# Three of the 48 output-weight rows of a partition are loaded on their own by small DMAs, and the score sums are taken two chunks at a time

## The chip, the cores and the metric

One NeuronCore of a Trainium2 chip runs the kernel; the metric is device time of one execution in microseconds (us). The engines are PE (TensorE), DVE (VectorE), ACT (ScalarE), POOL (GpSimd) and SP (SyncE, which here only issues DMAs); sixteen DMA engines move the data. POOL and ACT can issue DMAs too.

## What is computed

One decoding step of a transformer block for 4 sequences: sliding-window attention over a cache, plus a gated feed-forward part, plus the input.

```python
x = A_x                                   # [4, 1, 640]
xn = _layernorm(x)
q = (xn @ wq)                             # 32 heads of 192
k, v = the last W = 2048 of 8192 cached positions, [4, 32, 2048, 192] each
p = softmax(q k^T * 192 ** -0.5)
attn = (p v, heads side by side) @ wo     # wo is [6144, 640]
ffn = (silu(xn @ w1) * (xn @ w3)) @ w2    # F = 1536
return x + attn + ffn
```

All inputs are bf16. The keys and values that are read are 201 MB of the 223 MB that the kernel reads.

## The kernel before

**Layout.** Partition p = 4 * head + r holds a quarter r of the window of one head. The window is cut into NU = 4 units of 512 positions, so a unit of keys or of values is one tile of 128 partitions x 128 positions x 192 numbers, 6 MB, 49,152 contiguous bytes a partition. `load` (L104 to L111) fetches such a tile by one DMA from SP into the pool `kv` of three buffers; the two last halves of values are fetched apart.

**Keys.** `keys` (L231) treats a unit in four chunks of 32 positions. DVE multiplies a chunk with the query (`mult`, L212, into one of two buffers `pr`), PE adds the 192 products down to 16 by twelve matmuls with the identity (`adder`, L219, into PSUM tile `ps`), and DVE sums the last 16 (`reduces`, L229). A list, `pend`, holds chunks whose last sum is still to be issued; `reduces` is called after the next chunk's product. After four units `chain` makes the softmax numbers.

**Values.** `values` (L264) spreads the weights into a tile `z` (DVE, L268) and multiplies it with the value tile on PE (L280). `evict` and `sort` (L288 to L298) bring a sequence's result into `oT`, [128 partitions, NI = 48, 32], the left operand of the output projection: partition p holds 48 of the 6144 rows of the attention result, and the same 48 rows of wo belong to it.

**Output weights.** Row i of partition p of wo is 640 numbers, 1,280 bytes. `wo_load` (L302) loads rows 38 to 47 into a `pr` buffer, and rows 0 to 25 and 26 to 37 (cuts 0, WM = 26, NI - WI = 38) into a `kv` buffer. `proj` (L312 to L316) adds two matmuls a row into the PSUM tile `acc`: rows 38 to 47 first, then 0 to 37.

**Feed-forward.** w1 and w3 are loaded and multiplied before the last values; w2 comes as the last three loads (8 rows, 3 rows, 1 row; L326), and its 24 matmuls (L423) are the last of PE. DVE adds the parts (L415, L416, L426), and two DMAs store the result.

**What sets the order.** PE and DVE each issue in the order of the program text (`ordered` adds the dependence). SP issues its DMAs in program order and waits in front of one until its buffer is free. `feed` issues one entry of the list `stream` for each unit that the main loop works off: cache units, then w1 and w3, the last values with wo rows 38 to 47, then the rest of wo and w2. So each of the sixteen DMA engines has a queue of SP's transfers and works through it in that order; a cache load gives each engine eight rows of 49,152 bytes.

**Start.** POOL makes the two identities and clears `oT` and others (L121 to L160), then loads x into `x_st` by two small DMAs (L125). DVE and ACT do the layer norm, and PE makes the queries as soon as wq has landed (L196, L205); ACT puts them into `qb` (L206).

The code of the functions concerned, with the profile's line numbers:

Of the kernel before, what the change touches and what calls it, by code (L numbers as in the profile page):

```python
# [10 lines left out]
FP32 = mybir.dt.float32  # L11
BF16 = mybir.dt.bfloat16
ALU = mybir.AluOpType
ACTF = mybir.ActivationFunctionType
AX = mybir.AxisListType
# [3 lines left out]
def kernel(  # L19
# [13 lines left out]
    CH: int = 32,  # L33
    R: int = 4,
    WI: int = 10,
    WM: int = 26,
    ALIGN: int = 64,
):


# [5 lines left out]
    nc = tc.nc  # L46
    P = 128
    B, Sq, D = A_x.shape
    _, H, Sk, Dh = A_k_cache.shape
# [3 lines left out]
    NJ = P  # L53
    NU = W // (NJ * R)
    NC = NJ // CH
    NK = Dh // DD
    SCALE = float(Dh) ** -0.5
    EPS = 1e-5
    NI = Dh // R
    NG = P // 32  # L60
    NH = H // NG
    QW = 2 * Dh
    NCH = 512
    DH = D // 2
# [11 lines left out]
    const = ctx.enter_context(tc.tile_pool(name="const", bufs=1))  # L76
    kvpool = ctx.enter_context(tc.tile_pool(name="kv", bufs=3))
    ppool = ctx.enter_context(tc.tile_pool(name="pr", bufs=2))
# [1 line left out]
    opool = ctx.enter_context(tc.tile_pool(name="o", bufs=1))  # L80
    small = ctx.enter_context(tc.tile_pool(name="small", bufs=2))
    ps_add = ctx.enter_context(tc.tile_pool(name="ps_add", bufs=2, space=MemoryType.PSUM))
    ps_o = ctx.enter_context(tc.tile_pool(name="ps_o", bufs=2, space=MemoryType.PSUM))
    ps_t = ctx.enter_context(tc.tile_pool(name="ps_t", bufs=3, space=MemoryType.PSUM))
    ps_acc = ctx.enter_context(tc.tile_pool(name="ps_acc", bufs=1, space=MemoryType.PSUM))

    ORDER_DEP = mybir.DependencyInfo(mybir.DependencyClass.NoSync, mybir.DependencyReason.SCHED_ONLY)
# [2 lines left out]
    def ordered(engine, inst):  # L90
        if engine in last:
            tc.add_manual_dep(inst.ins, last[engine].ins.name, ORDER_DEP, reason="issue order")
        last[engine] = inst
        return inst

    def dve(inst):
        return ordered("dve", inst)

    def pe(inst):
        return ordered("pe", inst)  # L100
# [3 lines left out]
    def load(which, b, s, n0=0, n1=NJ):  # L104
        if n0 == 0:
            kv = kvpool.tile([P, NJ, Dh], BF16, tag="kv")
            kvs[which, b, s] = kv
        p0 = Sk - W + s * NJ * R
        rows = {"k": A_k_cache, "v": A_v_cache}[which][b, :, p0:p0 + NJ * R, :].rearrange("h (r n) d -> h r n d", r=R)
        nc.sync.dma_start(out=kvs[which, b, s][:, n0:n1, :].rearrange("p n d -> p (n d)"),  # L110
                          in_=rows[:, :, n0:n1, :].rearrange("h r n d -> h r (n d)"))  # L111
# [8 lines left out]
    x_st = const.tile([64, DH], BF16, name="x_st")  # L120
    nc.gpsimd.memset(x_st[:], 0.0)  # L121

    def x_load():
        for t in range(2):
            nc.gpsimd.dma_start(out=x_st[32 * t:32 * t + B, :], in_=x_rows[:, t * DH:(t + 1) * DH])  # L125
# [7 lines left out]
    nc.sync.dma_start(out=wq1[:], in_=wq_rows[:, RV:KC, :])  # L133
    for s in range(2):
        load("k", 0, s)

    idb = const.tile([P, P], BF16, name="idb")
    make_identity(nc, idb[:])
    idf = const.tile([P, P], FP32, name="idf")
# [15 lines left out]
    at = (NH - 1) * NG * R  # L155
    for b in range(B):
        nc.vector.tensor_copy(out=qwin[:, b, at:at + NG * R].rearrange("p (g r) -> p g r", r=R),
                              in_=idf[:, b:P:32].unsqueeze(2).to_broadcast([P, NG, R]))
    oT = const.tile([P, NI, 32], BF16, name="oT")
    nc.gpsimd.memset(oT[:], 0.0)  # L160

# [23 lines left out]
    acc = ps_acc.tile([64, DH], FP32, name="acc")  # L185

    q_pss = []
    for k in range(NH // 2):
        pool, tag = (ps_add, "ps") if k < 2 else (ps_o, "o_ps")
        qp = pool.tile([P, 512], FP32, tag=tag)  # L190
        q_pss.append(qp)
    for kc in range(KC):
        wq = (wq0[:, kc, :] if kc < RV else wq1[:, 0, :]).rearrange("p (k g d) -> p k g d", g=NG, d=Dh)
        for k in range(NH // 2):
            for g in range(NG):
                pe(nc.tensor.matmul(q_pss[k][32 * g:32 * g + 32, 0:QW], lhsT=xnT[:, kc, :], rhs=wq[:, 2 * k:2 * k + 2, g, :],  # L196
                                    start=(kc == 0), stop=(kc == KC - 1)))
    for k in range(NH // 2):
        nc.scalar.copy(out=q_sb[:, 2 * k:2 * k + 2, :], in_=q_pss[k][:, 0:QW].rearrange("p (x d) -> p x d", x=2))
    qb = const.tile([P, B, Dh], BF16, name="qb")  # L200
    for b in range(B):
        bp = ps_t.tile([P, Dh], FP32, tag="t")
        for k in range(NH):
            w0 = (NH - 1 - k) * NG * R
            pe(nc.tensor.matmul(bp[:], lhsT=qwin[:, b, w0:w0 + P], rhs=q_sb[:, k, :], start=(k == 0), stop=(k == NH - 1)))  # L205
        nc.scalar.copy(out=qb[:, b, :], in_=bp[:])  # L206

    scs, es, rss, rcps, pend = {}, {}, {}, {}, []

    def mult(b, s, c):  # L210
# [2 lines left out]
                                    in1=qb[:, b, :].unsqueeze(1).to_broadcast([P, CH, Dh]), op=ALU.mult))  # L213
        return pr

    def adder(b, s, c, pr):
        ps = ps_add.tile([P, CH, DD], FP32, tag="ps")
        for kk in range(NK):
            pe(nc.tensor.matmul(ps[:], lhsT=idb[:], rhs=pr[:, :, kk * DD:(kk + 1) * DD], start=(kk == 0), stop=(kk == NK - 1)))  # L219
        pend.append((b, s, c, ps))  # L220

    def reduces():
        while pend:
            b, s, c, ps = pend.pop(0)
            if b not in scs:
                sc = small.tile([P, NU * NJ], FP32, tag="sc", bufs=1)
                scs[b] = sc
            at = s * NJ + c * CH
            dve(nc.vector.tensor_reduce(out=scs[b][:, at:at + CH], in_=ps[:], axis=AX.X, op=ALU.add))  # L229

    def keys(b, s):  # L231
        for c in range(NC):
            pr = mult(b, s, c)
            reduces()
            adder(b, s, c, pr)
# [55 lines left out]
    def sort(b):  # L291
        fp = ps_t.tile([P, NI], FP32, tag="t")
        o_ev = o_evs.pop(b)
        for c in range(R):
            for t in range(2):
                pe(nc.tensor.matmul(fp[:], lhsT=esel[:, t, R - 1 - c:R - 1 - c + P], rhs=o_ev[:, t, c * NI:(c + 1) * NI],  # L296
                                    start=(c == 0 and t == 0), stop=(c == R - 1 and t == 1)))
        nc.scalar.mul(out=oT[:, :, b:b + 1].rearrange("p i o -> p (i o)"), in_=fp[:], mul=rcps.pop(b)[:, 0:1])  # L298
# [3 lines left out]
    def wo_load(cuts, pool, tag, shape):  # L302
        wt = pool.tile(shape, BF16, tag=tag)
        flat = wt[:].rearrange("p a n -> p (a n)")
        for i0, i1 in zip(cuts, cuts[1:]):
            at = (i0 - cuts[0]) * D
            nc.sync.dma_start(out=flat[:, at:at + (i1 - i0) * D],
                              in_=A_wo.rearrange("(p i) n -> p i n", i=NI)[:, i0:i1, :].rearrange("p i n -> p (i n)"))
            for i in range(i0, i1):
                wos[i] = flat[:, at + (i - i0) * D:at + (i - i0 + 1) * D]  # L310

    def proj(i0, i1):  # L312
        for i in range(i0, i1):
            for t in range(2):
                pe(nc.tensor.matmul(acc[32 * t:32 * t + 32, :], lhsT=oT[:, i, :], rhs=wos[i][:, t * DH:(t + 1) * DH],  # L315
                                    start=(i == i0 and i0 == proj0), stop=(i == proj1)))  # L316
# [9 lines left out]
    def w2_load(i0, i1):  # L326
        if i0 == 0:
            ffn[2] = ffn["tile"][:, 2 * KC * F:2 * KC * F + NF * CF * D].rearrange("p (i n) -> p i n", n=D)
        nc.sync.dma_start(out=ffn[2][:, i0:i1, :], in_=B_w2.rearrange("(p i) n -> p i n", p=P)[:, i0:i1, :])
# [22 lines left out]
            pe(nc.tensor.transpose(out=hT_ps[:, c, :], in_=ffn["h"][0:32 * NF, c:NCH:CF], identity=idb[0:32 * NF, 0:32 * NF]))  # L352
        dve(nc.vector.tensor_copy(out=hT[:], in_=hT_ps[:]))

    proj0, proj1 = NI - WI, NI - WI - 1

    def last_values():
        for g in range(VS):
            load("v", B - 1, NU - 1, g * NJ // VS, (g + 1) * NJ // VS)
        wo_load((NI - WI, NI), ppool, "pr", [P, WI, D])  # L360

    def gates():
        ffn_load(1)
        ffn_load(3)

    def last_weights():
        wo_load((0, WM, NI - WI), kvpool, "kv", [P, NJ, Dh])
        for i0, i1 in ((0, (NF - 1) * CF), ((NF - 1) * CF, NF * CF - 1), (NF * CF - 1, NF * CF)):
            w2_load(i0, i1)

    units = [("k", 0, s) for s in range(NU)]
    for b in range(B):
        for s in range(NU):
            units += [("v", b, s)] + ([("k", b + 1, s)] if b < B - 1 else [])
    stream = [(load, u) for u in units[2:-1]] + [(gates, ()), (last_values, ()), (last_weights, ())]

    def feed():
        fn, args = stream.pop(0)
        fn(*args)

    feed()
    for which, b, s in units[:-1]:
        if which == "k":
            keys(b, s)
        else:
            if s == 0:
                reduces()
                chain(b)
            values(b, s)
        if stream:  # L390
            feed()
        if which == "k" and b > 0:
            reduces()
            if s == 0:
                rowsum(b - 1)
                if b == B // 2:
                    x_load()
            elif s == NU - 1:
                sort(b - 1)
        if which == "v" and s == NU - 1 and b < B - 1:  # L400
            evict(b)
        if which == "v" and s == 0 and b == B - 1:
            rowsum(b)
# [4 lines left out]
        values(B - 1, NU - 1, g * NJ // VS, (g + 1) * NJ // VS)  # L408
    evict(B - 1)
    sort(B - 1)  # L410
    proj(NI - WI, NI)
    proj(0, NI - WI)

    t1 = opool.tile([64, DH], BF16, tag="t1")
    dve(nc.vector.tensor_copy(out=t1[:], in_=acc[:]))  # L415
# [4 lines left out]
    for i in range(NF * CF):  # L420
        n, c = i // CF, i % CF
        for t in range(2):
            pe(nc.tensor.matmul(ff[32 * t:32 * t + 32, :], lhsT=hT[:, c, 32 * n:32 * n + 32], rhs=ffn[2][:, i, t * DH:(t + 1) * DH],  # L423
               start=(i == 0), stop=(i == NF * CF - 1)))
# [34 lines left out]
```

## Time and profile before

| what | us |
|---|---|
| median of 3 runs | 526.11 (526.09, 526.11, 526.54) |
| the profiled execution, its own time | 526.01 |
| its span, first to last instruction | 524.1 |
| PE busy | 341.9 (65%) |
| DVE busy | 300.5 (57%) |
| ACT busy | 17.8 (3%) |
| POOL busy | 4.7 (1%) |
| HBM read | 222.96 MB, 425 GB/s over the span |

The time outside the span is 526.01 - 524.1 = 1.9 us. In the page's second part the span is cut into 40 slices, with the busy share of an engine in tenths; the row DMA there is the mean share of the sixteen DMA engines. Its third part lists queues: q1 is what SP issues, q0 what POOL issues, q8 and q14 are instructions on their way to the engines. The chain of waits follows the end back to its causes. The trace also has every DMA packet: start, duration, queue and bytes, though not the number of the DMA engine that moved it; and for each DMA the sixteen times at which its completion semaphore was raised.

### The profile page before, as it was taken

To read this page: it belongs to the slowest core of one execution; us is meant where nothing else is said; L and a number is where in the kernel's file an instruction comes from. 1 tells how busy PE (TensorE), PEld (TensorE's weight loads), DVE (VectorE), ACT (ScalarE), POOL (GpSimd) and SP (SyncE) were. 2 spreads that over 40 slices of the span, in tenths; PEclk is the share of its full clock that TensorE was granted. 3 is DMA by queue.
4 is the path that set the end of the run, shared out by engine and by line. 5 is a ranking of instruction groups with operands and counts; after the bars stand their busy time and mean duration, and the time that the engine had idled before them with its cause. 6 is when DMAs were issued, how large, how long until landed. Compare 5 with 4: busy or idle time off the path is not lost.

```text
span 524.1 us, 4690 instructions
## 1 busy us (share of the span) xinstructions
PE 341.9 (65%) x2147; PEld 199.4 (38%) x2147; DVE 300.5 (57%) x189; ACT 17.8 (3%) x34; POOL 4.7 (1%) x13
## 2 busy tenths in 40 slices
PE   0507677667676776596675866686565867688447
PEld 0302233253524352363434342353324353475445
DVE  4018999876583937676564828675574839411200
ACT  2110000000000000000000000000000000001100
POOL 3000000000000000000000000000000000000000
PEclk9977999979897887889798887998797888888797
DMA  9999999999999999999999999999999999999995
GB/s 361 431 448 439 420 425 447 439 421 424 436 450 425 420 435 451 431 418 439 443 433 424 424 455 431 425 420 450 436 431 421 435 448 428 428 420 427 432 425 240
DMA packets 6299, 223.26 MB, mean 426 GB/s; under 512 B 756, under 2 KB 904, under 8 KB 1032
## 3 DMA queue, kind: packets, MB, share of 16 engines
q1 hardware_dynamic: 6200, 222.96, 98.6%
q8 instruction: 16, 0.26, 0.2%
q14 instruction: 3, 0.02, 0.0%
q0 software_dynamic: 64, 0.01, 0.0%
q10 hardware_dynamic: 16, 0.01, 0.0%
HBM read 222.96 MB, written 0.01 MB: 425 GB/s over the span
## 4 chain that ended last, share of the span: by engine, by line
DMA 43%; DVE 29%; PE 25%; issue 1%; ACT 1%; SPq 0%; DVEq 0%; ACTq 0%
DMA kv<-in_A_k_cache_dram 38%; DVE pr L212 21%; PE o_ps L280 12%; PE ps L219 9%; DMA wt<-in_A_wo_dram 6%; DVE z L268 4%; DVE sc L229 4%; PE acc L315 2%; PE fp L296 1%; ACT e L252 1%; PE ft L423 0%; PE mt L247 0%; DVE gmax L244 0%; DVE gmq L246 0%; PE mt L242 0%
## 5 line engine op out<-in xcount | busy, mean ns | idle before, releaser
L212 DVE TENSOR_TENSOR pr<-kv,qb 128x6144 bf16<-128x6144 bf16 x64 | 213.4, 3351 | 104.7 <-DMA kv<-in_A_k_cache_dram 104.7
L219 PE MATMUL ps<-pr,idb 128*128 128x512 bf16 x768 | 194.1, 409 | 96.8 <-DVE pr L212 96.8
L219 PEld LDWEIGHTS <-idb 128*128 128x128 bf16 x768 | 79.5, 104 | 208.6 <-issue 122.6
L280 PE MATMUL o_ps<-kv,z 128*64 128x384 bf16 x1024 | 115.1, 396 | 50.6 <-DVE z L268 45.4
L280 PEld LDWEIGHTS <-z 128*64 128x64 bf16 x1024 | 94.5, 197 | 70.6 <-DVE z L268 53.0
L229 DVE TENSOR_REDUCE sc<-ps 128x32 f32<-128x512 f32 x64 | 43.9, 687 | 47.3 <-PE ps L219 47.2
L268 DVE TENSOR_TENSOR z<-e,selz 128x4096 bf16<-128x4096 bf16 (+1 forms) x17 | 36.7, 2158 | 18.2 <-PE o_ps L280 14.5
L315 PE MATMUL acc<-wt,oT 128*32 128x320 bf16 x96 | 9.5, 371 | 6.7 <-DMA wt<-in_A_wo_dram 6.1
L415 DVE CAST t<-acc 64x320 bf16<-64x320 f32 x1 | 0.5, 483 | 22.3 <-PE acc L315 22.3
L288 ACT COPY o_ev<-o_ps 128x384 f32<-128x384 f32 x4 | 1.9, 479 | 289.5 <-PE o_ps L280 289.5
L196 PE MATMUL qp<-wq,xnT 128*32 128x384 bf16 x80 | 5.2, 440 | 7.9 <-DMA wq<-in_A_wq_dram 7.9
L315 PEld LDWEIGHTS <-oT 128*32 128x32 bf16 x96 | 6.5, 118 | 9.5 <-issue 7.0
L296 PEld LDWEIGHTS fp<-o_ev,esel 128*128 128x128 f32 x64 | 7.7, 192 | 1.3 <-ACT o_ev L288 0.9
L296 PE MATMUL fp<-o_ev,esel 128*128 128x48 f32 x64 | 7.6, 272 | 0.6 <-ACT o_ev L288 0.6
L344 DVE TENSOR_TENSOR t_bf<-sg,t_bf 96x512 bf16<-96x512 bf16 x1 | 0.4, 420 | 11.5 <-ACT t_bf L338 11.5
L180 PE MATMUL xnT_ps<-idb,scratch 4*128 4x4 bf16 x5 | 0.4, 178 | 9.9 <-DVE scratch L176 9.9
L196 PEld LDWEIGHTS <-xnT 128*32 128x32 bf16 x80 | 3.1, 128 | 9.8 <-issue 7.5
L252 ACT ACTIVATE e<-sc,negm 128x512 bf16<-128x512 f32 x4 | 2.9, 721 | 80.5 <-DVE negm L249 80.5
L259 DVE RECIPROCAL rcp<-tb 128x1 f32<-128x1 f32 x4 | 0.6, 160 | 7.4 <-PE tb L257 7.4
L298 ACT ACTIVATE oT<-fp,rcp 128x48 bf16<-128x48 f32 x4 | 1.9, 468 | 64.9 <-PE fp L296 64.9
L180 PEld LDWEIGHTS <-scratch 4*128 4x128 bf16 x5 | 0.3, 125 | 9.9 <-DVE scratch L176 9.9
L205 PE MATMUL bp<-scratch 128*128 128x192 bf16 x32 | 3.3, 245 | 0.3
(60 smaller groups left out, 48.1 us busy)
## 6 DMA issues: line engine op xcount, KB each, us to landing
kv<-in_A_k_cache_dram SPq DMA_DIRECT2D x16, 6144.0 KB, 28.2
kv<-in_A_v_cache_dram SPq DMA_DIRECT2D x15, 6144.0 KB, 27.3
wq<-in_A_wq_dram SPq DMA_DIRECT2D x1, 6144.0 KB, 17.4
kv<-in_A_v_cache_dram SPq DMA_DIRECT2D x2, 3072.0 KB
wt<-in_A_wo_dram SPq DMA_DIRECT2D x1, 4160.0 KB, 29.4
ft<-in_B_w_dram SPq DMA_DIRECT2D x2, 1920.0 KB, 18.2
wt<-in_A_wo_dram SPq DMA_DIRECT2D x1, 1920.0 KB
wt<-in_A_wo_dram SPq DMA_DIRECT2D x1, 1600.0 KB, 27.8
```

Source lines behind the costliest of these rows:

```text
L196: pe(nc.tensor.matmul(q_pss[k][32 * g:32 * g + 32, 0:QW], lhsT=xnT[:, kc, :], rhs=wq[:, 2 * k:2 * k + 2, g, :], start=(kc == 0), stop=(kc ...
L205: pe(nc.tensor.matmul(bp[:], lhsT=qwin[:, b, w0:w0 + P], rhs=q_sb[:, k, :], start=(k == 0), stop=(k == NH - 1)))
L212: dve(nc.vector.tensor_tensor(out=pr[:], in0=kvs["k", b, s][:, c * CH:(c + 1) * CH, :], in1=qb[:, b, :].unsqueeze(1).to_broadcast([P, CH, ...
L219: pe(nc.tensor.matmul(ps[:], lhsT=idb[:], rhs=pr[:, :, kk * DD:(kk + 1) * DD], start=(kk == 0), stop=(kk == NK - 1)))
L229: dve(nc.vector.tensor_reduce(out=scs[b][:, at:at + CH], in_=ps[:], axis=AX.X, op=ALU.add))
L252: nc.scalar.activation(out=e[:], in_=sc[:], func=ACTF.Exp, bias=negm[:, 0:1], scale=SCALE, accum_out=rs[:])
L268: dve(nc.vector.tensor_tensor(out=z[:].rearrange("p h (a j) -> p h a j", j=ZB), in0=es[b][:, at:at + n].rearrange("p (a j) -> p a j", j=ZB ...
L280: pe(nc.tensor.matmul(o_pss[b][64 * t:64 * t + 64, 0:2 * Dh], lhsT=zf[:, a:a + (2 * H - 1) * half + 1:half], rhs=vt[:, n0 + a:n0 + a + hal ...
L288: nc.scalar.copy(out=o_ev[:].rearrange("p t d -> p (t d)"), in_=o_pss.pop(b)[:, 0:2 * Dh])
L296: pe(nc.tensor.matmul(fp[:], lhsT=esel[:, t, R - 1 - c:R - 1 - c + P], rhs=o_ev[:, t, c * NI:(c + 1) * NI], start=(c == 0 and t == 0), sto ...
L298: nc.scalar.mul(out=oT[:, :, b:b + 1].rearrange("p i o -> p (i o)"), in_=fp[:], mul=rcps.pop(b)[:, 0:1])
L315: pe(nc.tensor.matmul(acc[32 * t:32 * t + 32, :], lhsT=oT[:, i, :], rhs=wos[i][:, t * DH:(t + 1) * DH], start=(i == i0 and i0 == proj0), s ...
```

## The change

- Rows 45 to 47 of every partition of wo (WX = 3) no longer come with the other rows. A new tile `wx` of [128, 2, 3 * 640] is cleared by POOL at the start. Sixteen small DMAs fill half of its partitions with two partitions' rows each: each DMA writes 4 partitions x 2 x 3,840 bytes. The first dimension of its access patterns has 4 entries.
- Eight of the sixteen (partitions 0 to 15 and 32 to 47) are issued by SP, one right behind each of eight cache loads. The other eight (partitions 80 to 95 and 112 to 127) are issued by POOL, behind ACT's last copy into `qb`.
- `proj_ends` is new: two matmuls with a permutation `swap` bring the rows of `oT` to the partitions where their weights are, ACT copies the result, and 12 matmuls add the three rows into `acc`. It stands between the first and the second `proj`.
- The other cuts move down: rows 35 to 44 in the `pr` buffer, 0 to 22 and 23 to 34 in the `kv` buffer (WM = 23).
- `adder` puts two chunks side by side into a tile of two PSUM banks, and one DVE sum covers both: 32 sums of 128x1024 for 64 of 128x512. `ps_add` keeps 2 buffers, now of two banks; `ps_o` goes from 2 buffers to 1 and `ps_t` from 3 to 2.

In the changed kernel PE has 8 matmuls more (4,160 for 4,144 rows of matmuls, weight loads and others), DVE has 156 instructions for 188, SP has 53 for 45.

```diff
-    WM: int = 26,
-    ALIGN: int = 64,
+    WM: int = 23,
+    WX: int = 3,
+    ALIGN: int = 192,
...
-    ps_o = ctx.enter_context(tc.tile_pool(name="ps_o", bufs=2, space=MemoryType.PSUM))
-    ps_t = ctx.enter_context(tc.tile_pool(name="ps_t", bufs=3, space=MemoryType.PSUM))
+    ps_o = ctx.enter_context(tc.tile_pool(name="ps_o", bufs=1, space=MemoryType.PSUM))
+    ps_t = ctx.enter_context(tc.tile_pool(name="ps_t", bufs=2, space=MemoryType.PSUM))
...
+    wx = const.tile([P, 2, WX * D], BF16, name="wx")
+    nc.gpsimd.memset(wx[:], 0.0)
+    wo_ends = A_wo.rearrange("(p i) n -> p i n", i=NI)[:, NI - WX:NI, :].rearrange("(y x h e q) i n -> y x q e h (i n)", y=2, x=2, h=2, e=4)
+    wx_rows = wx[:].rearrange("(y x h e q) h2 n -> y x h q e h2 n", y=2, x=2, h=2, e=4)
+
+    def wx_load(y, x, q, queue):
+        return queue.dma_start(out=wx_rows[y, x, y, q], in_=wo_ends[y, x, q])
...
+    swap = const.tile([P, 2, 4, 2, 16], BF16, name="swap")
+    for h in range(2):
+        nc.gpsimd.tensor_copy(out=swap[:, h], in_=idb[:].rearrange("p (a h r) -> p a h r", a=4, h=2)[:, :, h:h + 1, :].to_broadcast([P, 4, 2, 16]))
...
-        nc.scalar.copy(out=qb[:, b, :], in_=bp[:])
+        qcopy = nc.scalar.copy(out=qb[:, b, :], in_=bp[:])
+    behind_q = mybir.DependencyInfo(mybir.DependencyClass.Sync, mybir.DependencyReason.SCHED_ONLY)
+    for x in range(2):
+        for q in range(4):
+            di = wx_load(1, x, q, nc.gpsimd)
+            tc.add_manual_dep(di.ins, qcopy.ins.name, behind_q, reason="behind the short runs of the query weights")
...
-        ps = ps_add.tile([P, CH, DD], FP32, tag="ps")
+        if c % 2 == 0:
+            ps = ps_add.tile([P, 2, CH, DD], FP32, tag="ps")
+            adds[b, s] = ps
+        ps = adds[b, s]
         for kk in range(NK):
-            pe(nc.tensor.matmul(ps[:], lhsT=idb[:], rhs=pr[:, :, kk * DD:(kk + 1) * DD], start=(kk == 0), stop=(kk == NK - 1)))
-        pend.append((b, s, c, ps))
+            pe(nc.tensor.matmul(ps[:, c % 2], lhsT=idb[:], rhs=pr[:, :, kk * DD:(kk + 1) * DD], start=(kk == 0), stop=(kk == NK - 1)))
+        if c % 2 == 1:
+            pend.append((b, s, c - 1, ps))
...
-            dve(nc.vector.tensor_reduce(out=scs[b][:, at:at + CH], in_=ps[:], axis=AX.X, op=ALU.add))
+            dve(nc.vector.tensor_reduce(out=scs[b][:, at:at + 2 * CH], in_=ps[:].rearrange("p a j d -> p (a j) d"), axis=AX.X, op=ALU.add))
...
+    NM = NI - WX
+    oX = const.tile([P, 2, WX, 32], BF16, name="oX")
+
+    def proj_ends():
+        xp = ps_t.tile([P, 2, WX * 32], FP32, tag="t")
+        for o in range(2):
+            pe(nc.tensor.matmul(xp[:, o, :], lhsT=swap[:, o].rearrange("p a h r -> p (a h r)"),
+                                rhs=oT[:, NM:NI, :].rearrange("p i o -> p (i o)"), start=True, stop=True))
+        nc.scalar.copy(out=oX[:].rearrange("p o i b -> p (o i b)"), in_=xp[:].rearrange("p o n -> p (o n)"))
+        for o in range(2):
+            for i in range(WX):
+                for t in range(2):
+                    at = i * D + t * DH
+                    pe(nc.tensor.matmul(acc[32 * t:32 * t + 32, :], lhsT=oX[:, o, i, :], rhs=wx[:, o, at:at + DH],
+                                        start=False, stop=False))
...
-        wo_load((0, WM, NI - WI), kvpool, "kv", [P, NJ, Dh])
+        wo_load((0, WM, NM - WI), kvpool, "kv", [P, NJ, Dh])
...
+    ends = [(0, x, q, nc.sync) for x in range(2) for q in range(4)]
+
     def feed():
         fn, args = stream.pop(0)
         fn(*args)
+        if ends and len(stream) < len(units) - NU:
+            wx_load(*ends.pop(0))
...
-    proj(NI - WI, NI)
-    proj(0, NI - WI)
+    proj(NM - WI, NM)
+    proj_ends()
+    proj(0, NM - WI)
```

More of the change, by code (lines that the diff above doesn't have):

```diff
@@ L187 @@
     q_pss = []
[L188 to L191, printed above, removed]
+    for k in range(0, NH // 2, 2):
+        qp = ps_add.tile([P, 2, 512], FP32, tag="ps")
+        q_pss += [qp[:, 0, :], qp[:, 1, :]]
     for kc in range(KC):
@@ L214, in mult @@
         return pr
+    adds = {}
     def adder(b, s, c, pr):
-        ps = ps_add.tile([P, CH, DD], FP32, tag="ps")
+        if c % 2 == 0:
+            ps = ps_add.tile([P, 2, CH, DD], FP32, tag="ps")
+            adds[b, s] = ps
+        ps = adds[b, s]
         for kk in range(NK):
-            pe(nc.tensor.matmul(ps[:], lhsT=idb[:], rhs=pr[:, :, kk * DD:(kk + 1) * DD], start=(kk == 0), stop=(kk == NK - 1)))
-        pend.append((b, s, c, ps))
+            pe(nc.tensor.matmul(ps[:, c % 2], lhsT=idb[:], rhs=pr[:, :, kk * DD:(kk + 1) * DD], start=(kk == 0), stop=(kk == NK - 1)))
+        if c % 2 == 1:
+            pend.append((b, s, c - 1, ps))
     def reduces():
@@ L353, in ffn_transpose @@
         dve(nc.vector.tensor_copy(out=hT[:], in_=hT_ps[:]))
-    proj0, proj1 = NI - WI, NI - WI - 1
+    NM = NI - WX
[12 more added lines that the diff above has]
+                                        start=False, stop=False))
+    proj0, proj1 = NM - WI, NM - WI - 1
     def last_values():
@@ L359, in last_values @@
             load("v", B - 1, NU - 1, g * NJ // VS, (g + 1) * NJ // VS)
-        wo_load((NI - WI, NI), ppool, "pr", [P, WI, D])
+        wo_load((NM - WI, NM), ppool, "pr", [P, WI, D])
     def gates():
```

## The prediction

> **What bounds the kernel now.** I read the page's overview first, then the DMA queues, then the end of the time line, and last the single DMA packets.
>
> ```profile
> DMA  9999999999999999999999999999999999999995
> ...
> q1 hardware_dynamic: 6200, 222.96, 98.6%
> q8 instruction: 16, 0.26, 0.2%
> q14 instruction: 3, 0.02, 0.0%
> q0 software_dynamic: 64, 0.01, 0.0%
> ```
>
> All sixteen DMA engines are busy in every slice but the last; PE is busy 65%, DVE 57%. Less work on DVE or PE gains nothing by itself. SP's cache loads are queued early enough: the tightest is issued at 117.23 us, when the first DMA engine has still 5.2 us of the load before (its completion counts run from 122.44 to 124.66).
>
> The time line at the end (start, duration, engine, line, operation):
>
> ```profile
> 503.85 1.53 PE L315 MATMUL acc<-wt,oT 128*32 128x320 bf16 x20 [0.65 <-ACT oT L298]
> 511.45 7.95 PE L315 MATMUL acc<-wt,oT 128*32 128x320 bf16 x76 [6.07 <-DMA wt<-in_A_wo_dram]
> 519.23 1.80 PE L423 MATMUL ft<-ft,hT 128*32 128x320 bf16 x24
> ```
>
> PE starts its last 100 matmuls when wo rows 0 to 25 land (last completion 511.41). The first 40 start 133 ns apart (PEclk 0.5 until 516.81), the others 68 ns apart; the last pair starts at 520.72, and `res` on DVE follows at 521.07. The last DMA, one row of w2, ends its last packet at 520.31 and completes at 520.62, 0.10 us before PE uses it. DMA and PE thus end almost together; both hang on the slowest DMA engine.
>
> **The sixteen engines are not equal.** On one engine a packet starts 3 to 4 ns before the one before it ends, so the packets can be strung into sixteen rows (numbers are mine, in order of the first packet; two rows that tie at 7.96 us stay open). A 49,152-byte packet takes 1.815 us on every row, without a pause. What differs are the instruction fetches: the sixteen 16,384-byte ones (q8, at every 250 or so of PE's instruction records) fall on eight rows, two each. One costs 0.96 us plus 0.47 in the next packet (2.28 for 1.815), 1.43 in all. Two of 8,192 bytes (q14, at 90.27 and 435.49) both fall on row 6 and cost 0.31 + 0.53 = 0.84 each. Last packets end so:
>
> ```
> 7 rows without a fetch   516.62 516.74 516.79 516.82 517.12 517.35 517.48
> row 6, two of 8,192 B    519.10
> 8 rows, two of 16,384 B  519.56 519.74 519.80 519.81 520.03 520.13 520.15 520.31
> ```
>
> So seven engines stand idle for up to 3.7 us at the end. The change has to be judged by which rows its bytes move to.
>
> **Part by part.**
>
> 1. *Three rows less in the big loads.* Each engine loses 8 x 3,840 bytes. Packets of 33,280 and 15,360 bytes start 1.229 and 0.569 us apart, 0.0368 ns a byte: 8 x 0.141 = **-1.13 us on all sixteen rows**.
> 2. *SP's eight DMAs.* Four entries in the first dimension: if, like the x load, each uses four engines, those get 16 packets of 3,840 bytes (0.146 us start to start in w2's packets) and 8 closing ones of 6 ns: **+2.38 us on four rows**.
> 3. *POOL's eight.* No such DMA is in the trace; the nearest rows are POOL's two `x_st` loads, also four partitions each: every packet of 640 bytes took 0.03 us and the cache packet behind it its usual 1.815. Lower bound per packet 0.146, upper bound that of a fetch in between, 0.5 more, which would be +8 us. I take 0.146, since a POOL packet showed no such penalty: +2.38 on four rows. Each `x_st` load also put two 4-byte packets (6 ns) on the other twelve rows: 8 x 2 x 6 ns = +0.10.
> 4. *Which four.* The 640-byte packets of both `x_st` loads lie on rows 2, 3, 6 and one of 4 and 7: the same four twice, three surely among the eight without PE fetches. So POOL's bytes go to rows that have room, row 6 among them. For SP's four the trace shows nothing; I take four of the other fetch-free rows.
> 5. *Row 6's second fetch.* Its two come when DVE alone (beside PE) is working, 132 DVE records apart; 8,192 bytes in steps of 64 are 128 instructions. DVE records 213 now; 32 sums fewer leave 181, and the second came at 184. It then falls behind the last work: **-0.84 on row 6**.
>
> Sum of row ends: PE's eight 520.31 - 1.13 + 0.10 = 519.28; row 6 519.10 - 1.13 - 0.84 + 2.38 = 519.51; SP's four at most 517.48 - 1.13 + 2.38 + 0.10 = 518.83. Row 6 is last: 519.51, 0.80 earlier. Completion 0.31 later is 519.82; the last pair waits for it and starts 0.04 later, 519.86 for 520.72: **-0.86 us**. PE must be there: rows 0 to 22 land at 510.21 - 1.13 - 0.84 + 2.38 = 510.62 (row 6's count of that DMA), start 510.66; 94 matmuls for 100 need 9.27 - 6 x 0.068 = 8.86, so 519.52, covered by 0.34 us. Should the slow clock last 6.83 us from there (the clock's rows last 3.41 or 6.83), PE's last pair would start at 520.3 and the gain be 0.45.
>
> **Costed at nothing.** The clear of `wx`: `oT` (1,536 a partition) took 1.37 us and `scratch` (960) 0.89, so 3,840 take some 3.3 us ahead of the identities and the layer norm; PE waits 7.9 us for wq there, which hides it. POOL's issues (0.6 us each) start at 27.3, with nothing behind them. SP's small DMAs wait for the clear and for semaphores of DMAs long landed; behind them stand only cache loads with 5 us of room. The early rows get 2.4 us later, which that room covers. `proj_ends`, some 0.5 us on ACT (a 128x384 copy takes 0.48) and 14 matmuls, falls into PE's 6.07 us of waiting. DVE's sums:
>
> ```profile
> L229 DVE TENSOR_REDUCE sc<-ps 128x32 f32<-128x512 f32 x64 | 43.9, 687 | 47.3 <-PE ps L219 47.2
> L244 DVE TENSOR_REDUCE gmax<-mt 1x32 f32<-1x128 f32 x4 | 1.1, 278 | 1.8 <-PE mt L242 1.8
> ```
>
> By these two rows 1.07 ns an element: some 1.23 us for 1,024, 32 of them 39 us for 44. A unit's last sum ends 0.5 us later; DVE waits 104.7 us for DMA in all, so neither counts. With one `o_ps` buffer the next sequence waits for the evict, with a unit of keys in between.
>
> The profiled 526.01 gives 525.15; the runs' median lies 0.10 higher: **525.25**.
>
> **Rivals.**
>
> - *POOL's four wander.* Then each row gets a quarter of its 2.38, 0.60, and 0.07 of small packets: PE's eight end at 520.31 - 1.13 + 0.67 = 519.85, -0.46: 525.65. Against it: both `x_st` loads on the same rows. [...]
> - *A fetch stays or a new one comes on row 6* (DVE's, or SP's with its 8 more DMAs: one q14 fetch came at 523.0, behind all work, where SP was busy). Row 6 ends at 520.35: 526.1, no change.
> - *Row 6 isn't among POOL's four after all.* PE's eight decide, 519.28; -1.09: 525.0.
> - *Slower: SP's four are among PE's eight.* They end at up to 520.31 - 1.13 + 0.10 + 2.38 = 521.66, complete at 521.97, the pair starts at 522.01: +1.29, 527.4. It decides as soon as one such row lies above 519.51, which all eight would. Much like it: SP's and POOL's four are the same, row 6 at 521.90: 527.6. For it: nothing in the trace places SP's four, and half of the rows carry PE's fetches. Against it: the rows that fetch and the rows that POOL uses are each a fixed set, three of POOL's four surely outside PE's eight, which looks like groups that were laid out and not like chance.
>
> **How the numbers follow.** Forecast 0.47, wandering 0.12, fetch 0.14, row 6 free 0.10, slower 0.17. A measurement of this kernel can tell about 0.2%, 1.05 us, from no change. Faster by more: row 6 free (0.10) and the forecast's upper edge, where the small packets cost less than I take (0.08): 0.18. Slower by more: 0.17. Within: 0.65. The range leaves out the slower cases and little else: 524.9 to 526.4.
>
> **What would show it.** Right: the packets of 3,840 bytes on eight rows that carry no 16,384-byte fetch; one q14 fetch of 8,192 bytes before 520 us; last packets of the rows between 518 and 519.6; PE's second `acc` group starting near 510.7. Wrong: 3,840-byte packets on a row with a fetch, a second q14 fetch ahead of the end, or a DMA share below 0.9 anywhere before 500 us, which would mean that a wait of SP let the queues run dry.

## The result and the profile after

The changed kernel takes 528.16 us (median of 6 runs, 527.50 to 528.67), the kernel before 526.12 beside it: ratio **1.0037 [1.0024, 1.0050]**, 2.0 us slower. The forecast was 525.25, the range up to 526.4. The profiled execution took 528.60, its span is 526.1 for 524.1. Two of the ten runs of experiment 3 below took near 541.5 us, in a slower state of the chip, and are left out of its time and ratio.

From the page of the changed kernel, the overview and the queues, and two groups (count | busy us, mean ns | idle us ahead of them):

```profile
span 526.1 us, 4717 instructions
...
DMA  8999999999999999999999999999999999999995
GB/s 359 441 399 427 416 424 422 456 427 425 426 451 425 425 442 443 422 428 435 437 431 430 441 431 437 427 441 434 427 430 438 437 430 431 434 428 421 425 429 242
...
q1 hardware_dynamic: 6296, 222.71, 98.5%
q8 instruction: 16, 0.26, 0.2%
q0 software_dynamic: 320, 0.25, 0.2%
q14 instruction: 3, 0.02, 0.0%
...
L250 DVE TENSOR_REDUCE sc<-ps 128x64 f32<-128x1024 f32 x32 | 39.1, 1222 | 36.9 <-PE ps L239 36.9
...
L130 POOL DMA_DIRECT2D wx<-in_A_wo_dram x8 | 4.6, 586 | 19.6 <-ACT qb L216 19.6
```

The DMA engines are about as busy as before and move the same bytes, yet they finish later. The third slice (26 to 39 us) has 399 GB/s, before 448. The time line's end (start, duration) shows where it arrives:

```profile
513.55 3.30 PE L336 MATMUL acc<-wt,oT 128*32 128x320 bf16 x46 [0.28 <-DMA wt<-in_A_wo_dram]
518.06 1.81 PE L336 MATMUL acc<-wt,oT 128*32 128x320 bf16 x24 [1.21 <-DMA wt<-in_A_wo_dram]
521.12 1.94 PE L465 MATMUL ft<-ft,hT 128*32 128x320 bf16 x24 [1.25 <-DMA ft<-in_B_w_dram]
```

PE now waits for weights three times. Its second `acc` group starts at 513.55, where 510.7 was forecast, and w2's last packet ends at 522.39 for 520.30 before: +2.09, which is the span's +2.0. So the loss is in the DMA engines. One pair of windows finds it; columns: the window and its length, busy us (and count) of PE, weight loads, DVE, ACT and POOL, granted clock, DMA share, GB/s. The kernel before, 31 to 61 us:

```profile
31.00:61.00 30.00, 15.78 (x60) 6.43 (x61) 21.32 (x10) 0.00 (x0) 0.00 (x0) 0.77 1.01 436
```

and the changed kernel:

```profile
31.00:61.00 30.00, 15.69 (x58) 6.39 (x59) 19.83 (x8) 0.00 (x0) 2.51 (x5) 0.72 1.00 401
```

The DMA share is 1.01 and 1.00, the rate 436 and 401: the engines were at work all the time, but slower. In the single packets, 112 of the 254 cache packets that start between 31 and 62 us took over 1.865 us instead of 1.815, up to 2.30, and they are on all sixteen rows. Summed over the run, cache packets exceed 1.815 us by 1.36 us a row before and 3.15 after: **+1.79 us on the average row**. (Between 31 and 62 us alone it is 1.94, against nothing before; the rest of the run has 0.15 less.) These long packets lie beside POOL's packets, which come in eight turns of four (7,680 bytes each: two rows in one packet). The excess of the cache packets around each turn, each packet counted once, summed over all rows:

```
turn       1      2      3      4      5      6      7      8
start us   33.4   35.2   39.4   43.8   47.2   51.1   53.4   57.9
excess us  3.64   4.37   6.07   0.05   5.46   6.14   5.20   0.07
```

Turns 4 and 8 cost nothing; the other six do. That pattern made the theories.

### The profile page after: what moved, and what is told of

Its sections match the earlier page's. It is cut to its first block, busy times and chain, and to the rows that moved or that the text cites. A ratio compares the mean times of both kernels' runs of the same rounds, so it can differ in the third digit from the quotient of the medians.

```text
span 526.1 us, 4717 instructions
## 1 busy us (share of the span) xinstructions
PE 339.8 (65%) x2155; PEld 200.2 (38%) x2155; DVE 298.6 (57%) x157; ACT 18.1 (3%) x35; POOL 13.4 (3%) x24
## 4 chain that ended last, share of the span: by engine, by line
DMA 50%; DVE 27%; PE 19%; issue 2%; ACT 0%; SPq 0%; DVEq 0%; another core or an unknown queue 0%; ACTq 0%
DMA kv<-in_A_k_cache_dram 38%; DVE pr L227 20%; PE o_ps L301 10%; PE ps L239 8%; DMA ft<-in_B_w_dram 7%; DMA kv<-in_A_v_cache_dram 6%; DVE sc L250 4%; DVE z L289 3%; ACT e L273 0%; DVE lmax L261 0%; PE ft L465 0%; PE mt L268 0%; DVE gmax L265 0%; PE mt L263 0%; SPq L328 0%
## 5 line engine op out<-in xcount | busy, mean ns | idle before, releaser
L239 PE MATMUL ps<-pr,idb 128*128 128x512 bf16 x768 | 189.4, 402 | 96.1 <-DVE pr L227 96.1
L239 PEld LDWEIGHTS <-idb 128*128 128x128 bf16 x768 | 77.6, 102 | 205.0 <-issue 77.7
L301 PEld LDWEIGHTS <-z 128*64 128x64 bf16 x1024 | 96.9, 198 | 75.1 <-DVE z L289 57.6
L250 DVE TENSOR_REDUCE sc<-ps 128x64 f32<-128x1024 f32 x32 | 39.1, 1222 | 36.9 <-PE ps L239 36.9
L336 PE MATMUL acc<-wt,oT 128*32 128x320 bf16 x90 | 8.0, 337 | 2.1 <-DMA wt<-in_A_wo_dram 1.5
L130 POOL DMA_DIRECT2D wx<-in_A_wo_dram x8 | 4.6, 586 | 19.6 <-ACT qb L216 19.6
```

Of the source, the lines that this page charges most:

```text
L130: return queue.dma_start(out=wx_rows[y, x, y, q], in_=wo_ends[y, x, q])
L239: pe(nc.tensor.matmul(ps[:, c % 2], lhsT=idb[:], rhs=pr[:, :, kk * DD:(kk + 1) * DD], start=(kk == 0), stop=(kk == NK - 1)))
L250: dve(nc.vector.tensor_reduce(out=scs[b][:, at:at + 2 * CH], in_=ps[:].rearrange("p a j d -> p (a j) d"), axis=AX.X, op=ALU.add))
L301: pe(nc.tensor.matmul(o_pss[b][64 * t:64 * t + 64, 0:2 * Dh], lhsT=zf[:, a:a + (2 * H - 1) * half + 1:half], rhs=vt[:, n0 + a:n0 + a + hal ...
```

## The experiments

Three theories of what costs the time. **A**: each turn goes to the next of four groups of four DMA engines, and what costs is a packet to partitions that are not the engine's own in a cache load. As the own partitions A assumes 0 to 15 and 32 to 47 for group 0, then 16 to 31 and 48 to 63, 64 to 79 and 96 to 111, and 80 to 95 and 112 to 127 for group 3, the one place to which all POOL's rows go. **B**: POOL's queue as such costs the time. **C**: a row that is set back by 0.3 us runs into conflicts with the others. Each excess below is per row over the whole run, to be read against 1.36 before.

**1. ACT issues POOL's eight DMAs.**

```diff
-            di = wx_load(1, x, q, nc.gpsimd)
+            di = wx_load(1, x, q, nc.scalar)
```

> POOL's eight small DMAs are issued by ACT instead, to the same partitions 80 to 95 and 112 to 127. Theory A (writes by a DMA engine to partitions that are not its own in the big loads slow all sixteen): ACT's data goes by the same four engines as SP's, whose own partitions are 0 to 15 and 32 to 47, so the cache packets behind them still stretch, 1.8 us a row between 30 and 60 us. Theory B (POOL's queue itself is the cause): no stretch, 1.815 us a packet. Both: the four rows carry twice 2.38 us, the row with the two 8,192-byte fetches ends at 519.1 - 1.1 + 4.8 = 522.7, which is 528.5 by B and about 530.3 by A.

Measured 532.5 us (four runs, 531.08 to 536.47), ratio 1.0135 [1.0089, 1.0180]; the profiled execution took 531.08, its span is 529.3; excess 4.85. The changed kernel's slow stretch only ended at 61 us; here the window from 31 to 75 us has

```profile
31.00:75.00 44.00, 24.80 (x100) 10.26 (x101) 34.06 (x13) 1.28 (x1) 0.00 (x0) 0.84 1.00 395
```

against 430 before. It is not POOL's queue: B falls as it stands. ACT's 64 packets of 3,840 bytes come one at a time in 21 rounds, and none of the full rounds was quiet. The end fits four rows that carry both SP's and ACT's packets. The row with SP's packets and DVE's fetch ends at 521.88 in the changed kernel; with ACT's 2.38 for the 0.67 of POOL's turns, and the longer stretch, it should end at 521.88 + 2.38 - 0.67 + (4.85 - 3.15) = 525.29. The last packet ends at 525.28.

**2. POOL's eight on own partitions; 3. on group 0's.** Both leave out SP's eight, and so half of the three rows' product. In run 2 each of POOL's DMAs goes to the partitions of the group whose turn it is by A: 0, 1, 2, 3, and again.

```diff
-            di = wx_load(1, x, q, nc.gpsimd)
+            i = 4 * x + q
+            di = nc.gpsimd.dma_start(out=wx_rows[i % 4 // 2, i // 4, i % 2, 0], in_=wo_ends[1, x, q])
...
-    ends = [(0, x, q, nc.sync) for x in range(2) for q in range(4)]
+    ends = []
```

> [...] Theory A: no stretched cache packets, HBM rate above 425 GB/s from 30 to 60 us, rows with PE fetches last at 520.31 - 1.13 + 0.67 = 519.85, 525.65 us. Theory B, and theory C (a shift of a row by 0.3 us alone brings the rows into step in HBM): six or more of the eight rounds stretched as in the changed kernel, 1.8 us a row, 527.4 us.

> As the run before it (SP's small DMAs left out, output not the reference's), but all eight POOL DMAs write to partitions 0 to 15 and 32 to 47. Theory A: the quiet rounds are the first and the fifth instead of the fourth and the eighth, six rounds are stretched, 527.4 us. Theory B: all or the same rounds stretched as in the changed kernel, whatever the partitions. Theory C: the fourth and the eighth stay quiet.

In run 3 the destination is `wx_rows[0, x, 0, q]` throughout. Run 2 measured 525.60, ratio 0.9990 [0.9980, 0.9999]; excess 1.20. Run 3 measured 527.56, ratio 1.0030 [1.0020, 1.0040], its profiled execution 526.98; excess 2.85. The same window in run 2:

```profile
31.00:61.00 30.00, 15.18 (x60) 6.26 (x61) 22.07 (x9) 0.00 (x0) 2.64 (x5) 0.78 0.99 428
```

and in run 3:

```profile
31.00:61.00 30.00, 15.40 (x60) 6.31 (x61) 21.38 (x8) 0.00 (x0) 1.03 (x2) 0.77 0.99 403
```

The packets are of one size, of one queue and at about the same times; only the partitions differ. In run 2 all eight turns are quiet (at most 0.01 us around each, beside one packet behind a fetch of PE, 0.48) and every packet of 7,680 bytes takes 291 or 292 ns. In run 3 the quiet turns are the first and the fifth (0.01 and 0.03; the others 2.6 to 5.3), as A had said, for group 0's turns. C falls with run 2, where the same shifts cost nothing.

**4. SP's half alone.** POOL's eight, and their half of the product, are left out.

```diff
-    for x in range(2):
-        for q in range(4):
-            di = wx_load(1, x, q, nc.gpsimd)
-            tc.add_manual_dep(di.ins, qcopy.ins.name, behind_q, reason="behind the short runs of the query weights")
```

> POOL's eight small DMAs are left out (half of the three rows' products is missing), SP's eight stay. All theories: no stretch, since SP's write to the partitions that its four engines write anyway. PE's eight rows end at 520.31 - 1.13 = 519.18. If the row with the 8,192-byte fetches is one of SP's four, it ends at 519.10 - 1.13 + 2.38 = 520.35 and the time is 526.1; if it is not, SP's four end below 518.8 and the time is 525.0.

Measured 525.24, ratio 0.9985 [0.9976, 0.9995], span 523.4; excess 1.29. w2's last packet ends at 519.44. The rows without a fetch and without SP's packets end at 515.76, 515.89, 516.14 and 516.24; the seven of before less 1.13 are 515.5 to 516.35. The time is neither of the two that I had named: DVE's row is one of SP's four, but its second fetch now comes behind its last packet (see part 5 below).

**5. SP's half on the partitions of POOL's half.** It differs from the changed kernel by the edit of run 4 and by this one:

```diff
-        return queue.dma_start(out=wx_rows[y, x, y, q], in_=wo_ends[y, x, q])
+        return queue.dma_start(out=wx_rows[1, x, 1, q], in_=wo_ends[y, x, q])
```

> The run with SP's half alone, its eight DMAs at the same places of SP's queue and on the same four engines, but written to the partitions that POOL's half has in the changed kernel (80 to 95 and 112 to 127); POOL's eight are left out, and so is their half of the three rows' product, while SP's rows are multiplied at the wrong place. A: the stretch comes to SP's queue and to 124 to 230 us. In the run with ACT in POOL's place 64 packets of 3840 bytes to foreign partitions cost each row 3.5 us; here there are as many: 525.24 + 3.5 = 528.7, at least 527.5, with cache packets over 1.9 us only behind these eight. B and C, or a stretch that needs a second queue beside SP's: 525.2 as on their own partitions.

Measured 527.76, ratio 1.0032 [1.0019, 1.0045]; excess 3.10. The window that holds the eight, in run 4:

```profile
120.00:230.00 110.00, 76.35 (x453) 43.84 (x452) 68.39 (x32) 1.76 (x4) 0.00 (x0) 0.88 1.01 436
```

and in run 5:

```profile
120.00:230.00 110.00, 75.52 (x430) 42.65 (x430) 65.34 (x32) 1.76 (x4) 0.00 (x0) 0.84 1.00 427
```

So the stretch follows the partitions to a third queue and another time: 1.6 to 4.4 us, summed over the rows, at each of the eight DMAs, where run 4 has at most 0.5. But the excess over before, 1.74 us a row, is half of the 3.5 that I expected. The price isn't one per packet or per byte: the run with ACT paid 3.5 us a row for 64 single packets of 3,840, this one 1.74 for 32 pairs of them, the changed kernel 1.79 for 24 packets of 7,680. Multiplied by 16 rows and shared out, that is 0.87, 0.87 and 1.2 us for each time that an engine turns to such rows.

**6. The sums alone.** The kernel before, with only `adder`, `reduces` and the PSUM buffers of the change. Of this edit, the line of the sum:

```diff
-            dve(nc.vector.tensor_reduce(out=scs[b][:, at:at + CH], in_=ps[:], axis=AX.X, op=ALU.add))
+            dve(nc.vector.tensor_reduce(out=scs[b][:, at:at + 2 * CH], in_=ps[:].rearrange("p a j d -> p (a j) d"), axis=AX.X, op=ALU.add))
```

> The kernel before with only the summing changed: two chunks to one sum of DVE (32 instead of 64) and the PSUM buffers that go with it; the weight rows are all loaded as before, and the product is the whole one. Both theories, that foreign writes cost the time (A) and that the extra queue does (B), expect no change: 526.1 within 0.3, DVE some 4 us less busy, cache packets at 1.815 us on all rows. If the two-chunk sums cost something by themselves (PE waiting for the larger buffer), it shows here as a time above 526.5.

Measured 526.00 beside 526.00, ratio 0.9999 [0.9991, 1.0008]. Its page:

```profile
PE 339.4 (65%) x2147; PEld 198.9 (38%) x2147; DVE 298.5 (57%) x157; ACT 17.8 (3%) x34; POOL 4.7 (1%) x13
...
L234 DVE TENSOR_REDUCE sc<-ps 128x64 f32<-128x1024 f32 x32 | 39.0, 1220 | 36.9 <-PE ps L223 36.9
```

The sums are 4.9 us cheaper (43.9 before), DVE in all 2.0; the end doesn't move.

**7. The whole change with every row of POOL's queue on own partitions.** Nothing is left out. POOL issues eleven DMAs, three of them from the first half for group 0's turns, and SP five; `swap` gets the columns that fit. The edit, in part:

```diff
+    turns = [(0, 0, 0), (1, 0, 0), (1, 0, 1), (1, 0, 2), (0, 0, 1), (1, 1, 0), (1, 1, 1), (1, 1, 2), (0, 0, 2), (1, 0, 3), (1, 1, 3)]
+    for i, (y, x, q) in enumerate(turns):
+            g = i % 4
+            di = nc.gpsimd.dma_start(out=wx_rows[g // 2, x, g % 2, q], in_=wo_ends[y, x, q])
...
-    ends = [(0, x, q, nc.sync) for x in range(2) for q in range(4)]
+    ends = [(0, x, q, nc.sync) for x in range(2) for q in range(4)][3:]
```

> The whole change, nothing left out, but every row of GpSimd's queue is written to partitions that the DMA engine whose turn it is also writes in the cache loads: eleven DMAs of GpSimd in the turn of the four groups (three of them carry rows of the first half, for the turns of group 0), five of SP, and a product matrix that puts the rows back. A: no stretched cache packets; the rows with PE's fetches get -1.13 + 3 x 0.29 = -0.25 us against before and group 0, which has none, +1.25, so the last rows end 0.25 us earlier than before: 525.85, within 0.4. B (any DMA of that queue among the cache loads stretches them) or C (the shift of a row stretches them): as after, 527.5 to 528.2. That the whole change on these partitions isn't slower than before would settle that the partitions make the loss.

Measured 525.68 beside 526.00, ratio 0.9996 [0.9987, 1.0005]; span 523.8, excess 1.18, the longest cache packet between 31 and 62 us 1.821 us. The window, and the end of its time line:

```profile
31.00:61.00 30.00, 15.80 (x60) 6.42 (x61) 21.13 (x8) 0.00 (x0) 3.35 (x6) 0.77 0.99 429
```

```profile
511.11 7.81 PE L344 MATMUL acc<-wt,oT 128*32 128x320 bf16 x70 [3.26 <-DMA wt<-in_A_wo_dram]
518.77 1.85 PE L473 MATMUL ft<-ft,hT 128*32 128x320 bf16 x24
```

w2's last packet ends at 519.99; PE's rows were reckoned at 520.31 - 1.13 + 3 x 0.29 = 520.05. The loss of the changed kernel is gone, with all its loads and its product in place: the partitions make it. That leaves it level with the kernel before; I found no version that is faster by more than the measurement can tell and computes everything.

## Why the prediction was wrong

- *Part 1, -1.13 us on all rows*: right (run 4's free rows).
- *Part 2, SP's +2.38 on four rows without PE's fetches*: right as to PE's fetches. The packet strings of the changed kernel put SP's on the same four rows eight times, none with a 16,384-byte fetch; but one of them is the row of DVE's fetch (121.61 us, SP's first packet 3 us later). No stretch: run 4's excess is 1.29, for 1.36 before. By luck SP's rows go to partitions that don't cost (run 5, on POOL's partitions, has 3.10): the prediction did not look at partitions.
- *Part 3, "I take 0.146, since a POOL packet showed no such penalty"*: **the step that failed.** The nearest row, `x_st`'s 640 bytes, was of one kind only: it goes to partitions 0 to 3 and 32 to 35, which A counts to group 0, and at least three of its four rows are rows that carry SP's packets in the changed kernel. The upper end that I named, 0.5 us behind each packet on its own row, had the wrong form too: the packet itself costs its 0.146 a row (291 ns for two), and what it costs besides, 1.2 us for each of the 24 that go to other partitions, is spread over all sixteen rows: 1.79 us a row, where the prediction had nothing. I had named no price for rows that carry no such packet.
- *Part 4, "the same four twice"*: wrong. The four wander: in the packet strings of the changed kernel a row that takes part in one turn does so again four turns later (for turns 1 to 4 one row each: at 33.37 and 47.24 us, 35.22 and 51.12, 40.07 and 54.13, 44.12 and 58.42). Runs 2 and 3 agree (at most 0.01 us at any of run 2's eight turns, and the quiet ones of run 3 four turns apart). Why the two `x_st` loads stayed on the same rows no run shows. So that rival had the rows right, with its +0.67 on all of them (0.60 and 0.07); its 525.65 lacked the stretch.
- *Which partitions cost.* The own partitions that A assumed fit all these runs: on them run 2 has at most 0.01 us a turn and run 7 no cache packet over 1.821 us, on others the changed kernel and runs 1, 3 and 5 have 0.87 to 1.2 us a visit (run 3: (2.85 - 1.36) x 16 / 24 = 0.99). What makes the partitions matter, and why engines without such packets are slowed, none of the runs shows.
- *Part 5, the vanished fetch*: right for DVE, wrong for the kernel. Packets of 8,192 bytes on q14:

```
                          SP's small DMAs   within the loads         next
before                    0                 90.27, 435.49            523.01
run 6, sums alone         0                 117.39                   519.91
runs 2 and 3              0                 117.84 / 120.15          518.90 / 520.40
changed kernel            8                 121.61, 479.48           521.88
run 1                     8                 123.17, 484.80           525.29
runs 4 and 5              8                 117.40, 475.97 / 117.16, 481.88   519.45 / 520.98
run 7                     5                 120.05, 486.73           520.15
```

  Without half of the sums DVE's second one comes 130 of its records after the first, now at the end. The step of 64 bytes, an estimate, fits the trace of before: a fetch of 16,384 bytes comes at every 254 of PE's records on average, 64.5 bytes a record, and 8,192 bytes over 132 of DVE's are 62. The count behind the step was off, though: DVE has 197 records and not 181, and its second fetch did come, at the 192nd, directly behind the last packet of its row; the step held, but not by its own count. Only kernels with SP's small DMAs have one near 480, when SP is at its 81st to 83rd record: it is SP's, the rival's "a new one". In the changed kernel it lies on one of PE's rows, not on row 6. In run 4 the row of DVE's fetch should end at 519.10 - 1.13 - 0.84 + 2.38 = 519.51 if the new one lies on another row there too, and 0.84 later if not; the last packet ends at 519.44.
- *The sum.* The row that carries SP's packets and DVE's fetch should end at 519.51, which by chance is the number forecast for row 6, + 0.67 (POOL's turns) + 1.79 (stretch) = 521.97. It ends at 521.88, with DVE's next fetch directly behind it, and is not the last.

  The last packets, up to 522.39, are on one of PE's rows, the one that was last before as well (its second fetch is at 303.80 us before and at 307.02 after). Its part of w2 takes 4.66 us without a pause, as on every other row, so no late fetch holds it up. The forecast for it was 519.28, so 3.11 us are missing: 0.57 are the turns (0.67 for 0.10), and 2.54 are left for the stretch. All of its delay is there by 62 us: from then up to 470 us its packets start 3.22 us later than in the kernel before. Reckoned in the same way the stretch of PE's other seven rows is 1.2 to 2.0 us. Why the last row got more than those isn't shown. Part of it can come from the start of the run, ahead of POOL's packets: the rows begin their tenth packet of 49,152 bytes up to 1 us apart (22.39 to 23.38 us), and not in the same way in every run. Without the stretch, 521.97 would be 520.18 and the last row near 519.85, for 520.31 before: no loss, as run 7 then showed.
- *Costed at nothing*: right. The sum of 1,024 elements a partition took 1,222 ns (1.23 us estimated), run 6 shows that the sums don't move the end, and in run 7 clear, `proj_ends` and POOL's issues are all present in a kernel no slower than before.
- *Rivals*: the slower one came near in time (527.4) for the wrong reason; in the changed kernel SP's four are not among PE's eight.

## What to carry to other kernels

In a kernel whose sixteen DMA engines are all busy, a small transfer is judged by which engine moves it and to which partitions: here eight DMAs of 30 KB cost 1.8 us on the average of all sixteen rows, and next to nothing when every engine wrote partitions that it also writes in the large loads (excess 1.20 in run 2 and 1.18 in run 7, for 1.36 before). DMA share near 1 at a lower rate (401 GB/s for 436 in the same window) is the sign to look for. The nearest operation in a trace bounds the cost only of what it has in common with the new one; a small load that by A stays within group 0 (`x_st`'s, 1.815 us for each cache packet behind it) said nothing about one to others.

## What the runs showed of the hardware

- Packets of 3,840 or 7,680 bytes to partitions other than the engine's own slowed the cache packets of all sixteen rows, also those that carried none in the same turn of four (112 of 254 cache packets over 1.865 us between 31 and 62 us, on all rows): in sum 1.2 us for each visit from POOL's queue (the changed kernel), 0.87 from ACT's (run 1) and 0.87 from SP's (run 5). On own partitions it was at most 0.01 us around each turn (run 2, beside one packet behind a fetch) and at most 0.5 us around each of SP's DMAs (run 4).
- POOL's eight DMAs of four entries moved on to other rows each time and were back at the same four every fourth turn (44.12 and 58.42 us on one row of the changed kernel; quiet turns 4 and 8 there, 1 and 5 in run 3). SP's stayed on the same four rows, eight times in the changed kernel; ACT's, by the end of the last row (525.28 us for 525.29 reckoned), used SP's four.
- Eight (in run 7 five) more DMAs in SP's program brought a fetch of 8,192 bytes between 475.97 and 486.73 us, which the kernels without them do not have.
